# Letting two of the four row groups of a score block start before the running exponential ends, in a scheduled attention plus gated-MLP kernel

## The chip, the cores and the metric

One core of a Trainium2 chip. The metric is the device time of one execution in microseconds (us), as the median of several. Engine names: TensorE (PE in the profile, its weight loads PEld), ScalarE (ACT), VectorE (DVE), GpSimd (POOL), SyncE (SP). In the views, S_ps is the PSUM space of the scores, F_ps that of every other matmul, Pr the probabilities, tnh the outputs of tanh. A wide matmul is one that streams 512 columns.

## The reference, cut to what matters

A transformer layer on 2048 tokens of width 1024: 32 query heads of 32 dimensions share one key head and one value head; then a gated MLP of width 3584.

```python
q = (ln(x) @ wq)            # 2048 x 1024, 32 heads of 32
k, v = ln(x) @ wk, ln(x) @ wv                  # one head each, 2048 x 32
p = softmax(q @ k.T / sqrt(32))                # 32 heads x 2048 x 2048
h = x + (p @ v) @ wo
g, u = ln(h) @ w_gate, ln(h) @ w_up            # 2048 x 3584
out = h + (sigmoid(g) * u) @ w_down            # sigmoid by a tanh on ScalarE
```

## The kernel before

The kernel is written through a list scheduler. Each operation is recorded with the operations that it depends on, an estimated occupancy and latency; the scheduler puts TensorE's work in one fixed order, and the others' with it. On the chip only that order and the semaphore waits exist; the estimates are gone.

The attention part is cut into 512 *score blocks*, 32 for each tile of 128 queries. A block is eight matmuls: four row groups `j` of the array, which run together and hold two heads each, and two rounds `kk` of 128 keys. Six PSUM banks serve the scores as three pairs. Row groups 0 and 1 of block `v` fill one pair and row groups 2 and 3 the next; each pair is read by one exponential of 1024 columns on ScalarE, number `u` = 2v or 2v+1. (The recorded texts below say heads where they mean row groups.)

```python
def t_act(n):                                # the scheduler's idea of a ScalarE instruction
    return dict(occ=n / 1.2 + 53.0, lat=n / 1.2 + 170.0 + SEM)

# s_ready(v): what block v waits for
    deps = [q_ready[qb][g], q_ready[qb][g + 1], k_ev[kq]]
    if 2 * v - 2 >= 0:
        deps.append(exps[2 * v - 2])
    ...
# emit_S(v)
    for kk in range(KB):                     # 2
        for j in range(4):
            bank = 2 * ((2 * v + j // 2) % NB) + j % 2        # NB = 3 pairs
            last = pl.op("pe", mm(S_ps[:, bank, ...], kT4[...], QTb[...], True, True, tile_position=(DH * j, 0)),
                         deps if (kk == 0 and j == 0) else [], occ=27.4, lat=27.4 + 150.0 + SEM)
    for i in range(2):
        u = 2 * v + i
        exps[u] = pl.op("act", ... ACT.activation(out=pslot(slot)..., in_=S_ps[:, pb:pb + 2, :], func=Exp), [last] + free, ...)

# the main loop: a score block goes out when it can, and when ScalarE has under 750 ns of work left
    can_s = sd is not None and known(sd, t)
    if can_s and run - t < 750.0:
        emit_S(v); v += 1
        if pv_fits():
            emit_PV(t)                       # probabilities times values, in column-tiled mode
    # otherwise: matmuls of the projections and of the MLP fill TensorE's time
```

Row groups 0 and 1 of block `v` use the pair that exponential 2v-3 read; row groups 2 and 3 the pair of exponential 2v-2. The whole block waits for 2v-2, while 2v-1 is still running.

The softmax here doesn't subtract the row's maximum and nothing guards it: scores larger than these inputs give would overflow.

## Time and profile before

| | before |
|---|---|
| median | 1092.27 us at first (1091.58 to 1092.71), 1092.13 with the later run |
| ScalarE busy, 581 to 643 us (about one query tile) | 62.00 of 62.00 us |
| end-to-end distance of exponentials | 916.7 ns (mean, 200 to 985 us) |
| period of a query tile | 62.10 us |
| last exponential ends | 1016.5 us |
| rest after it | 72.8 us |

The windows view of the kernel before gives the busy time of each engine in a stretch; the number in brackets counts instructions. The first stretch is one query tile of attention, the second lies in the tail.

```profile
core 0: us, PE busy (x) PEld busy (x) DVE busy (x) ACT busy (x) POOL busy (x), PEclk, DMA share, GB/s
581.00:643.00 62.00, 59.93 (x749) 26.54 (x760) 54.49 (x102) 62.00 (x72) 1.19 (x2) 1.00 0.76 202
1020.00:1089.00 69.00, 65.94 (x328) 29.81 (x326) 15.33 (x28) 4.78 (x8) 0.79 (x2) 1.00 0.78 203
```

ScalarE has no idle time in the first stretch. In the tail it does almost nothing, and TensorE sets the time. The timeline of ScalarE (start, length, then what, and how many instructions were merged) tells its real pace:

```profile
610.92 7.64 ACT L670 ACTIVATE Pr<-S_ps 128x1024 bf16<-128x1024 f32 x8
618.27 0.77 ACT L948 ACTIVATE tnh<-F_ps 128x512 f32<-128x512 f32 x1
618.75 5.80 ACT L670 ACTIVATE Pr<-S_ps 128x1024 bf16<-128x1024 f32 x6
```

Read the ends, not the starts. The eight exponentials end at 610.92 + 7.64 = 618.56, the tanh at 619.04, the next six at 624.55. So a tanh adds about 0.49 us, and an exponential (624.55 - 619.04) / 6 = 0.918 us. The starts overlap the instruction before: the tanh starts 0.29 us before the last of the eight has ended. Unrounded, a tile holds 64 x 0.9167 + 7 x 0.490 = 62.10 us of ScalarE, and the chain of waits repeats every 62.1 us:

```profile
447.98 6.41 ACT Pr L670 x7
510.07 6.42 ACT Pr L670 x7
572.17 6.42 ACT Pr L670 x7
634.26 6.42 ACT Pr L670 x7
```

The waits view of the kernel before (who waited for whom: us in total, times, longest) names the score blocks' wait as a large one:

```profile
PEld S_ps L393 <- ACT Pr L670: 165.8, 388, 0.6
PEld S_ps L393 <- ACT tnh L948: 34.3, 81, 0.4
PEld S_ps L393 <- issue: 14.2, 40, 0.5
```

That is idle time of the weight-load lane, not of the matmuls. Most of it is the 216 ns in which the last wide matmul still streams, and the drain of the array, a further 96 ns between a matmul in another tiling mode and row-tiled ones. From the start of the last wide matmul to the start of the block it takes 311 or 312 ns in 357 of the 475 blocks that follow a wide matmul. Only 103 of the 512 blocks start more than 10 ns later than that, by 9.0 us in all. The counts in this document that no view prints (these waits, end distances, periods) are sums over the records of single instructions.

### The profile page before, as it was taken

The numbers are of one execution on the slowest core, as the hardware profiler recorded it, in microseconds if no ns is written. First come the engines' busy times: TensorE is split into PE (matmuls) and PEld (weight loads), VectorE is DVE, ScalarE is ACT, GpSimd is POOL, SyncE is SP. The second block draws the span as 40 slices with busy tenths as digits, with TensorE's granted clock in tenths as the row PEclk, the third lists the DMA queues.
The fourth block names the chain that finished last, engine by engine and source line by source line (L and its number), as shares of the span: only waits on it lengthen the run. The fifth ranks groups of instructions, "written<-read, shape, count | busy, mean of one in ns | idle before, by whom it ended". The sixth has DMA issues, their size and how long they took to land.

```text
span 1089.3 us, 31275 instructions
## 1 busy us (share of the span) xinstructions
PE 1046.4 (96%) x12757; PEld 481.2 (44%) x12931; DVE 910.2 (84%) x1756; ACT 1006.6 (92%) x1164; POOL 28.5 (3%) x58
## 2 busy tenths in 40 slices
PE   8999999999999999999999999999999999999998
PEld 5664444444444444444444444444444444444443
DVE  8789988898888889798888989898888979888611
ACT  6899999999999999999999999999999999999310
POOL 2100000000000000000000000000000000000000
PEclk9999999999999999999999999999999999999999
DMA  9996599949688694949789594968869494967993
GB/s 251 194 310 221 141 282 256 279 104 281 163 216 231 158 267 113 278 123 261 190 195 256 125 277 106 275 161 235 211 167 260 126 271 115 278 170 196 283 263 89
DMA packets 310991, 228.18 MB, mean 209 GB/s; under 512 B 121920, under 2 KB 302144, under 8 KB 310848
## 3 DMA queue, kind: packets, MB, share of 16 engines
q1 hardware_dynamic: 308768, 226.04, 79.7%
q8 instruction: 102, 1.67, 0.7%
q10 hardware_dynamic: 2080, 0.13, 0.1%
q14 instruction: 41, 0.34, 0.1%
HBM read 195.69 MB, written 7.86 MB: 187 GB/s over the span
## 4 chain that ended last, share of the span: by engine, by line
ACT 47%; PE 31%; issue 10%; DVE 10%; DMA 1%; POOL 0%; SPq 0%; DVEq 0%
ACT Pr L670 41%; PE F_ps L393 27%; ACT tnh L948 5%; DVE Ts L704 5%; PE S_ps L393 5%; DVE Rc L766 1%; DVE h_sb L834 1%; DVE st L334 1%; DVE hact L284 1%; DMA ring<-in_B_w_up_dram 1%; DVE Rc L771 0%; DMA zone<-ring 0%; DMA ring<-in_A_x_dram 0%; DVE Ri L769 0%; ACT wo_sb L670 0%
## 5 line engine op out<-in xcount | busy, mean ns | idle before, releaser
L670 ACT ACTIVATE Pr<-S_ps 128x1024 bf16<-128x1024 f32 x1012 | 962.6, 1177 | 5.9 <-PE S_ps L393 5.8
L704 DVE TENSOR_TENSOR Ts<-Ts,Pr 128x1024 bf16<-128x1024 bf16 x732 | 480.2, 679 | 38.1 <-ACT Pr L670 34.2
L393 PE MATMUL F_ps<-ring,hnT 128*128 128x512 bf16 (+1 forms) x2046 | 411.7, 380 | 19.3 <-issue 12.8
L393 PEld LDWEIGHTS F_ps<-ring,hnT 128*128 128x128 bf16 (+1 forms) x2153 | 156.2, 97 | 194.7 <-issue 50.5
L393 PE MATMUL F_ps<-zone,hact 128*128 128x512 bf16 (+1 forms) x1046 | 212.2, 380 | 7.1 <-issue 4.3
L393 PE MATMUL S_ps<-QTb,kT 32*128 32x256 bf16 x4096 | 203.3, 273 | 3.5 <-ACT Pr L670 0.7
L393 PEld LDWEIGHTS S_ps<-QTb,kT 32*128 32x128 bf16 x4096 | 61.0, 92 | 214.7 <-ACT Pr L670 165.8
L393 PE MATMUL F_ps<-Pr,Vb 128*32 128x256 bf16 x4048 | 134.3, 274 | 0.0
L948 ACT ACTIVATE tnh<-F_ps 128x512 f32<-128x512 f32 x112 | 86.8, 775 | 45.4 <-PE F_ps L393 45.4
L393 PEld LDWEIGHTS F_ps<-zone,hact 128*128 128x128 bf16 (+1 forms) x1088 | 80.9, 97 | 98.6 <-issue 19.6
L704 DVE TENSOR_TENSOR Ts<-Pr 128x1024 bf16<-128x1024 bf16 x126 | 85.9, 683 | 45.0 <-ACT Pr L670 45.0
L393 PEld LDWEIGHTS F_ps<-Pr,Vb 128*32 128x32 bf16 x4048 | 96.3, 96 | 29.9 <-issue 19.0
L952 DVE SCALAR_TENSOR_TENSOR hst<-tnh,F_ps 128x512 bf16<-128x512 f32 x112 | 76.6, 684 | 28.9 <-PE F_ps L393 28.9
L393 PE MATMUL F_ps<-zone 128*128 128x256 bf16 (+4 forms) x574 | 73.5, 274 | 4.3 <-DVE hact L284 1.2
L393 PE MATMUL F_ps<-wo_sb,OT 128*128 128x512 bf16 (+1 forms) x373 | 60.2, 379 | 2.6 <-issue 2.4
L393 PEld LDWEIGHTS F_ps<-zone 128*128 128x128 bf16 (+1 forms) x583 | 41.9, 97 | 27.6 <-issue 9.2
L982 DVE SCALAR_TENSOR_TENSOR h_sb<-F_ps,h_sb 128x512 bf16<-128x512 f32 x32 | 22.1, 692 | 36.4 <-PE F_ps L393 36.4
L711 DVE TENSOR_TENSOR Ts<-Ts 128x1024 bf16<-128x1024 bf16 x64 | 43.9, 686 | 1.5
L348 POOL TENSOR_SCALAR zb<-mvb 128x1 bf16<-128x1 bf16 (+1 forms) x25 | 11.2, 446 | 999.3 <-DVE mvb L344 999.3
L393 PEld LDWEIGHTS F_ps<-wo_sb,OT 128*128 128x128 bf16 (+1 forms) x388 | 22.8, 97 | 26.4 <-issue 6.3
L754 DVE TENSOR_TENSOR Oc<-F_ps,Oc 128x256 f32<-128x256 f32 x60 | 25.4, 424 | 7.0 <-PE F_ps L393 4.5
L771 DVE STREAM_TRANSPOSE Rc<-Ri 128x256 f32<-128x256 f32 x64 | 28.1, 438 | 0.0
(64 smaller groups left out, 345.0 us busy)
## 6 DMA issues: line engine op xcount, KB each, us to landing
ring<-in_B_w_gate_dram SPq DMA_DIRECT2D x320, 256.0 KB, 4.3
ring<-in_B_w_up_dram SPq DMA_DIRECT2D x320, 256.0 KB, 4.3
zone<-in_B_w_down_dram SPq DMA_DIRECT2D x28, 256.0 KB, 3.5
h_sb<-in_A_x_dram SPq DMA_DIRECT2D x16, 256.0 KB, 4.9
out_dram<-h_sb SPq DMA_DIRECT2D x32, 128.0 KB, 3.0
ring<-in_A_x_dram SPq DMA_DIRECT2D x7, 512.0 KB, 6.6
QTb<-q_scratch SPq DMA_DIRECT2D x14, 256.0 KB, 4.2
q_scratch<-hact SPq DMA_DIRECT2D x16, 128.0 KB, 3.1
```

The lines of the kernel that those rows point to most:

```text
L284: lambda: DVE.tensor_copy(out=out_ap, in_=in_ap))
L334: a = pl.op("dve", lambda k=k, src=src: DVE.bn_stats(st[:, k, 0, :], src[:, 0:512]), dep, prio=prio, occ=590, lat=756, order=[st_user.get(k)])
L348: f = pl.op("pool", lambda: POOL.tensor_scalar(out=zb[:, ph, sl].unsqueeze(2), in0=mvb[:, ph, sl, 1:2], scalar1=LN_EPS_BF16, scalar2=None, ...
L393: fn = lambda: PE.matmul(o, lhsT=l, rhs=r, start=start, stop=stop, **kw)
L670: exps[u] = pl.op("act", lambda slot=slot, pb=pb: ACT.activation(out=pslot(slot).rearrange("p (a b) -> p a b", a=2), in_=S_ps[:, pb:pb + 2 ...
L704: o = pl.op("dve", lambda T=T, a=a, b=b: DVE.tensor_tensor(out=T, in0=a, in1=b, op=ALU.add), deps, prio=4, **t_dve(1024, 1.92))
L711: merge_ev[G] = pl.op("dve", lambda T4=T4: DVE.tensor_tensor(out=T4[:, :, 0, :], in0=T4[:, :, 0, :], in1=T4[:, :, 1, :], op=ALU.add), [sum ...
L754: a = pl.op("dve", lambda: DVE.tensor_tensor(out=Oc[:, :], in0=O, in1=Ob, op=ALU.add), [last, oc_ev[G], o_ev.get(G - 1)], prio=0, **t_dve( ...
L771: d = pl.op("dve", lambda: DVE.transpose(out=Rc[:, :], in_=Ri[:, :].unsqueeze(2).to_broadcast([P, 2 * P // DH, DH])), [r], prio=2, **t_dve ...
L948: tanh_of[n] = pl.op("act", lambda: ACT.activation(out=tnh[:, n % 2, :], in_=F_ps[:, b, :], func=ACTF.Tanh, scale=0.5), [last, tn_user.get ...
L952: e = pl.op("dve", lambda: DVE.scalar_tensor_tensor(out=hst[:, n % NST, :], in0=tnh[:, n % 2, :], scalar=1.0, in1=F_ps[:, b, :], op0=ALU.a ...
L982: e = pl.op("dve", lambda: DVE.scalar_tensor_tensor(out=h_sb[:, t % 4, sl], in0=F_ps[:, b, :], scalar=0.5, in1=h_sb[:, t % 4, sl], op0=ALU ...
```

## The change

The intent: the first two row groups need a pair of banks that was read long ago. They should go ahead while the exponential that holds the other pair still runs, and only the third matmul should wait. The scheduler may then send a block up to one drain time (92 to 100 ns by its table) before that exponential ends.

```diff
             deps = [q_ready[qb][g], q_ready[qb][g + 1], k_ev[kq]]
-            if 2 * v - 2 >= 0:
-                deps.append(exps[2 * v - 2])
+            if v > 1:
+                deps.append(exps[2 * v - 3])
@@ emit_S
-                                 deps if (kk == 0 and j == 0) else [], occ=27.4, lat=27.4 + 150.0 + SEM)
+                                 deps if (kk, j) == (0, 0) else [exps[2 * v - 2]] if (kk, j) == (0, 2) and v else [],
+                                 occ=27.4, lat=27.4 + 150.0 + SEM)
@@ main loop
-                can_s = sd is not None and known(sd, t)
+                can_s = sd is not None and known(sd, t) and (v == 0 or known([exps[2 * v - 2]], t + DRAIN[mode[0]]))
```

So there are two parts: semaphores that wait later within a block, and a scheduler rule that makes another order of nearly everything.

## The prediction

> **What bounds the kernel now.** Two engines in turn. Until about 1016.5 us ScalarE sets the pace. In the windows view of 581 to 643 us (one query tile) ScalarE is busy 62.0 of 62.0 us. The starts of exponentials hide the real pace: they lie 904 ns apart with small gaps, but the ends lie 916 to 917 ns apart, and an end after a tanh 490 ns later. The Trainium skill ("Perfetto Trace Analysis", DVE / Act Engine Instruction) says that the recorded end is the write's acknowledgement, so I take the ends; the trace agrees: 64 x 0.9166 + 7 x 0.490 = 62.09 us, and the tile period read from the score blocks is 62.09 us. So in steady state no exponential is late, though score blocks come only just in time. After the last exponential 72.8 us of matmuls remain (512 columns, 216 ns apart): TensorE sets the end. TensorE has work throughout; what it loses in the first part is paid in the tail.
>
> **What the change touches.** A score block follows its predecessor on TensorE by at least 312 ns (216 streaming, 96 drain). "TensorEngine Tiling (Array Packing)", Key Properties, says that a change of tiling mode drains the array; the trace agrees, 96 ns in 80% of blocks. So the weight loads' "wait for the exponential" (165.8 us in the waits view) is mostly drain, which stays. Real waiting beyond 312 ns is only 9 us over 103 of 512 blocks. An exponential just ended lets a block start about 56 ns later; the first two matmuls need only a much older one. But the third still waits for the same end, and the four row groups run together, so starting two early gains little for the block.
>
> The larger effect is that the kernel's list scheduler places blocks up to 96 ns earlier (mostly 35 ns, its 750 ns run-ahead rule binds) and reorders everything. Instruction order, before to after: filler matmuls 38 to 20 (18 x 109 ns, -2.0 us); mode changes 1036 to 1074, because PV groups now often follow full matmuls, not score blocks (about 38 x 0.1 us, +4 us). All transitions summed with measured spacings: TensorE +2.1 us in all. Per steady tile 61.07 becomes 61.39 us, still under ScalarE's 62.09. Work is the same 184 wide matmuls per tile. After the last score block 328 becomes 322 wide matmuls: -1.3 us. One more tanh (104 to 105) comes before the last exponential: +0.5 us.
>
> **Critical path.** The ScalarE period isn't touched, so most of TensorE's saved waiting doesn't count; what counts is the tail (-1.3), the tanh (+0.5) and the first 80 us, where ScalarE idles some 7 us in all and the new order is slightly shorter (-0.5, uncertain). Sum about -1.3 us.
>
> **Prediction: 1091.0 us, range 1087.0 to 1094.5. Chances: faster by over 2% 0.01, within 2% 0.97, slower 0.02.**
>
> **What the profile should show.** Tile period still 62.0 to 62.2 us; ends of exponentials 917 ns apart; drains still 96 ns; TensorE's waits beyond drain before score blocks lower than 9 us, or moved to the third matmul; last exponential within 2 us of 1016.5; tail 70 to 72.5 us; more full-to-column mode changes.
>
> **What would make it wrong.** PV groups now issued when probability slots run out could delay a score block past its slack of some 60 ns and starve ScalarE: period over 62.3 us and end distances over 930 ns. TensorE has only 0.7 us per tile of slack left; other losses (about 0.4 us) could use it up, adding up to 5 us. If the first 80 us lose much of the 7 us idle, it is faster by some 4 us. Weight loads, issued in another order, could stall a matmul by about 2 us, as twice before.

## The result, and the profile after

| | before | after |
|---|---|---|
| median | 1092.13 us (4 runs, 1091.58 to 1092.71) | 1092.05 us (4 runs, 1091.19 to 1092.85) |
| last exponential ends | 1016.5 us | 1019.3 us |
| rest after it | 72.8 us | 71.0 us |
| span of the profiled run | 1089.3 us | 1090.3 us |
| blocks that wait over 10 ns beyond the drain, first matmul | 93, 8.8 us | 1, 0.1 us |
| the same, third matmul | 0 | 110, 7.9 us |

(The row of the first matmul counts from 312 ns on for every block; the 103 blocks above were counted from 311 ns where a full matmul stood before the block, which takes in ten more. The row of the third counts what goes beyond its usual 3 ns after the second.)

The ratio is 0.9999, with a 95% interval from 0.9982 to 1.0016: the same. A ratio is the mean time of one kernel's runs over that of the other's of the same rounds, so it is not quite the ratio of the medians.

The windows view after, for the same stretches:

```profile
581.00:643.00 62.00, 61.94 (x750) 26.67 (x749) 53.78 (x103) 62.00 (x72) 0.79 (x2) 1.00 0.80 203
1020.00:1089.00 69.00, 67.35 (x379) 30.83 (x377) 16.76 (x31) 4.78 (x8) 0.79 (x2) 1.00 0.75 200
```

ScalarE is as full as before. TensorE's busy time seems to grow by 2 us a tile, but it does no more work: the trace of before lacks 174 of the program's 12931 matmul records, that of after none of 12721, and a missing record shows as idle time. In the stretch of before above there are 749 matmuls beside 760 weight loads. `sem_only2`, a run below with the order of before and all its records, shows this for the same stretch:

```profile
581.00:643.00 62.00, 61.82 (x761) 27.04 (x760) 54.61 (x102) 62.00 (x73) 1.19 (x2) 1.00 0.80 203
```

The tail's x328 against x379 is another matter: in after, the last PV group and its sums (36 matmuls) fall behind 1020 us. So neither the busy sum nor the page's chain (ScalarE 47% before, TensorE 86% after) tells of a new limit here; the chain is 90% TensorE in `sem_only2` too.

The timeline of ScalarE after:

```profile
611.36 6.75 ACT L671 ACTIVATE Pr<-S_ps 128x1024 bf16<-128x1024 f32 x7
617.81 0.80 ACT L949 ACTIVATE tnh<-F_ps 128x512 f32<-128x512 f32 x1
618.28 4.90 ACT L671 ACTIVATE Pr<-S_ps 128x1024 bf16<-128x1024 f32 x5
```

The ends are 618.11, 618.61 and 623.18: again 0.50 for the tanh and (623.18 - 618.61) / 5 = 0.914 us for an exponential, the same pace within the rounding. The mean end distance is 916.9 ns, and from the tenth tile on the period is 62.1 us.

The waits view after:

```profile
PEld S_ps L393 <- ACT Pr L671: 114.5, 291, 0.4
PEld S_ps L393 <- issue: 70.2, 187, 0.4
PEld S_ps L393 <- ACT tnh L949: 19.5, 46, 0.4
```

Some 56 us came to the line "issue" (14.2 before, 70.2 after), and the ScalarE lines lost 66 us (165.8 + 34.3 = 200.1 before, 114.5 + 19.5 = 134.0 after): the first weight load no longer has a ScalarE semaphore that came last. Most of the gap stays, because it is the stream and the drain: the three lines sum to 214.3 us before and 204.2 after.

What did change is the start. Before 150 us ScalarE lost 6.7 us between ends in the kernel before and 9.1 us in the kernel after. One stretch alone costs 3.3 us. TensorE's timeline after:

```profile
118.10 0.40 PE L393 MATMUL S_ps<-QTb,kT 32*128 32x256 bf16 x8
118.43 4.06 PE L393 MATMUL F_ps<-zone 128*128 128x512 bf16 x18
122.42 1.06 PE L393 MATMUL F_ps<-Pr,Vb 128*32 128x256 bf16 x32
123.30 0.28 PE L393 MATMUL F_ps<-Ts,ones 128*32 128x256 bf16 x4
123.52 0.40 PE L393 MATMUL S_ps<-QTb,kT 32*128 32x256 bf16 x8
```

and ScalarE's in the same place:

```profile
118.64 2.13 ACT L671 ACTIVATE Pr<-S_ps 128x1024 bf16<-128x1024 f32 x2
123.96 1.02 ACT L671 ACTIVATE Pr<-S_ps 128x1024 bf16<-128x1024 f32 x1 [3.19 <-PE S_ps L393]
```

The order has eighteen projection matmuls and a PV group between two score blocks, 5.4 us, where two exponentials last 1.8 us. In the order of before the same place holds seven projection matmuls, a score block, three more and the PV group:

```profile
117.47 1.68 PE L393 MATMUL F_ps<-zone 128*128 128x512 bf16 x7
119.09 0.40 PE L393 MATMUL S_ps<-QTb,kT 32*128 32x256 bf16 x8
119.64 0.59 PE L393 MATMUL F_ps<-zone 128*128 128x512 bf16 x2 [0.16 <-issue]
120.17 1.06 PE L393 MATMUL F_ps<-Pr,Vb 128*32 128x256 bf16 x32
```

(One of the three is among the missing records; `sem_only2`, with the same order, shows x3.)

### The profile page after: what moved, and what is told of

Read it like the earlier page. It is cut to its first block, busy times and chain, and to the rows that moved or that the text cites. A ratio compares the mean times of both kernels' runs of the same rounds, so it can differ in the third digit from the quotient of the medians.

```text
span 1090.3 us, 31042 instructions
## 1 busy us (share of the span) xinstructions
PE 1077.6 (99%) x12721; PEld 482.6 (44%) x12721; DVE 902.1 (83%) x1756; ACT 1007.3 (92%) x1164; POOL 23.6 (2%) x58
## 4 chain that ended last, share of the span: by engine, by line
PE 86%; ACT 8%; DVE 3%; issue 2%; DMA 1%; POOL 0%; SPq 0%; DVEq 0%
PE F_ps L393 72%; PE S_ps L393 14%; ACT Pr L671 7%; DMA ring<-in_B_w_up_dram 1%; ACT tnh L949 1%; DVE Ts L705 1%; DMA wo_sb<-in_A_wo_dram 0%; DMA ring<-in_A_x_dram 0%; DVE Rc L767 0%; DVE Oc L755 0%; DVE ring L373 0%; DVE ring L380 0%; DVE st L334 0%; DVE st L336 0%; DVE kT L284 0%
## 5 line engine op out<-in xcount | busy, mean ns | idle before, releaser
L393 PE MATMUL F_ps<-ring,hnT 128*128 128x512 bf16 (+1 forms) x1991 | 437.6, 380 | 3.0 <-issue 1.3
L393 PEld LDWEIGHTS F_ps<-ring,hnT 128*128 128x128 bf16 (+1 forms) x1991 | 153.0, 98 | 203.6 <-issue 58.9
L393 PE MATMUL F_ps<-zone,hact 128*128 128x512 bf16 (+1 forms) x1145 | 223.7, 380 | 0.0
L393 PE MATMUL S_ps<-QTb,kT 32*128 32x256 bf16 x4096 | 211.0, 273 | 0.4 <-ACT Pr L671 0.2
L393 PEld LDWEIGHTS S_ps<-QTb,kT 32*128 32x128 bf16 x4096 | 66.7, 92 | 202.9 <-ACT Pr L671 114.5
L393 PEld LDWEIGHTS F_ps<-Pr,Vb 128*32 128x32 bf16 x4048 | 96.4, 96 | 32.6 <-issue 17.6
L393 PE MATMUL F_ps<-zone 128*128 128x256 bf16 (+5 forms) x595 | 74.3, 277 | 4.1 <-DVE Vb L284 0.8
L393 PE MATMUL F_ps<-wo_sb,OT 128*128 128x512 bf16 (+1 forms) x289 | 66.7, 381 | 0.4 <-DMA wo_sb<-in_A_wo_dram 0.4
L348 POOL TENSOR_SCALAR zb<-mvb 128x1 bf16<-128x1 bf16 (+1 forms) x25 | 6.4, 255 | 1006.4 <-DVE mvb L344 1006.4
```

What stands on the lines that cost most here:

```text
L348: f = pl.op("pool", lambda: POOL.tensor_scalar(out=zb[:, ph, sl].unsqueeze(2), in0=mvb[:, ph, sl, 1:2], scalar1=LN_EPS_BF16, scalar2=None, ...
L393: fn = lambda: PE.matmul(o, lhsT=l, rhs=r, start=start, stop=stop, **kw)
```

## The experiments

My theory: ScalarE sets the pace of the attention part, so a block that starts earlier gains nothing; the wait only moves to the third matmul; the reorder costs or gains a little at the two ends. First rival: the early start is worth several us, and the worse order ate them. Second rival: TensorE sets the pace.

All runs of one group share their runs of the kernel before.

### One part at a time

`sem_only2` has the order of before on every engine, with only the semaphores moved:

```diff
-            deps = s_ready(v)
+            deps = [d for d in s_ready(v) if not (v and d is exps[2 * v - 2])] + ([exps[2 * v - 3]] if v > 1 else [])
-                                 deps if (kk == 0 and j == 0) else [], ...
+                                 deps if (kk, j) == (0, 0) else [exps[2 * v - 2]] if (kk, j) == (0, 2) and v else [], ...
```

> The instruction order of the kernel before on every engine, unchanged; only the wait moves: the first two matmuls of a score block wait for the older exponential, the third for the one in progress. Theory (ScalarE paces, the third matmul waits for the same end): 1092.1 us, within 1 us of before; some 90 waits, 8 to 9 us in all, now between the second and third matmul; tile period 62.09 us. Rival (starting two heads early gains, and the new order of the full change ate the gain): 5 to 9 us faster than before, about 1085 us, and the waits largely gone.

`order_only2` has the order of after on every engine, but each block waits whole:

```diff
-                                 deps if (kk, j) == (0, 0) else [exps[2 * v - 2]] if (kk, j) == (0, 2) and v else [],
+                                 deps + ([exps[2 * v - 2]] if v else []) if (kk, j) == (0, 0) else [],
```

> The instruction order of the kernel after on every engine, but every block waits whole, as before the change. Theory: same as after, 1092 us within 1 us; about 90 waits, 8 us, ahead of the first matmul. Rival (early start pays for a worse order): 4 us or more slower than after, 1096 us or more.

Measured: 1091.67 and 1091.52 us, beside 1091.40 us of the kernel before; ratios 1.0000 (0.9987 to 1.0012) and 1.0001 (0.9988 to 1.0014). With `sem_only2`, 122 third matmuls waited 9.3 us in all; with `order_only2`, 102 first matmuls waited 7.3 us. The first rival falls: moving the semaphores alone gains nothing, and undoing them in the new order costs nothing.

One block shows why. The two kernels have the same order, so the same block can be laid side by side. TensorE's timeline of before:

```profile
619.09 0.40 PE L393 MATMUL S_ps<-QTb,kT 32*128 32x256 bf16 x8
619.42 1.47 PE L393 MATMUL F_ps<-ring,hnT 128*128 128x512 bf16 x6
620.93 0.40 PE L393 MATMUL S_ps<-QTb,kT 32*128 32x256 bf16 x8
621.26 1.06 PE L393 MATMUL F_ps<-Pr,Vb 128*32 128x256 bf16 x32
```

and of `sem_only2`:

```profile
619.21 0.40 PE L393 MATMUL S_ps<-QTb,kT 32*128 32x256 bf16 x8
619.53 1.47 PE L393 MATMUL F_ps<-ring,hnT 128*128 128x512 bf16 x6
620.94 0.51 PE L393 MATMUL S_ps<-QTb,kT 32*128 32x256 bf16 x8
621.38 1.06 PE L393 MATMUL F_ps<-Pr,Vb 128*32 128x256 bf16 x32
```

All of `sem_only2` is 0.11 to 0.12 us later here. From the block before, the second block starts 1.84 us later in before and 1.73 us later in `sem_only2`, 0.11 us sooner. But it lasts 0.51 instead of 0.40 us, and the PV group behind it comes 2.17 us after the first block in both. By single records the eight matmuls of that block start at 0, 3, 7, 10, 120, 122, 127, 129 ns in before, and at 0, 4, 118, 121, 124, 128, 237, 241 ns in `sem_only2`. Two row groups run early; the other two and the second round come when they came before, and both exponentials wait for the last matmul of the block.

### More work for one engine

`pe_plus2` repeats the second round of four matmuls in every fourth block, unknown to the scheduler, so that the order stays:

```diff
+            for j in range(4 if v >= 96 and v % 4 == 0 else 0):
+                last = pl.op("pe", mm(<the matmul of kk = 1, row group j, once more>), [], occ=0.0, lat=150.0 + SEM)
```

> The kernel before with the second round of four score matmuls repeated in every fourth block from the fourth tile on (104 blocks, about 110 ns each, 11.4 us of TensorE time in all, 0.88 us a tile), in an otherwise unchanged order. Theory (ScalarE paces the attention part, TensorE waits about 0.9 us a tile): 0 to 3 us slower, tile period 62.1 to 62.3, TensorE's waits ahead of score blocks shrink from about 9 to under 4 us. Rival (TensorE paces): 11 us slower, period 62.9.

`act_plus2` adds a small copy on ScalarE after every eighth exponential:

```diff
+            if v >= 96 and v % 4 == 0:
+                pl.op("act", lambda: ACT.activation(out=scr[:, :], in_=ones[:, :], func=ACTF.Copy), [exps[2 * v], c_v1], prio=0, occ=0.0, lat=0.0)
```

> The kernel before with one small ScalarE copy (128x32) after every eighth exponential from the fourth tile on (104 of them), order otherwise unchanged. From the ends of exponential (916.6 ns, 1024 elements) and tanh (490 ns, 512) I estimate 63 ns fixed plus 0.83 ns an element, so 90 ns each, 9.4 us in all. Theory (ScalarE paces): 8 to 11 us slower, tile period 62.8. Rival (TensorE paces): under 3 us slower.

`act_plus2` took 1101.88 us against 1091.40 (ratio 1.0107, 1.0088 to 1.0126): 10.5 us more for 104 copies. (One of its four runs took 1106.11 us, at a granted clock of 0.998; it lifts the ratio above that of the medians.) Its ScalarE timeline:

```profile
611.28 6.83 ACT L671 ACTIVATE Pr<-S_ps 128x1024 bf16<-128x1024 f32 x7
617.80 0.42 ACT L676 ACTIVATE scr<-ones 128x32 bf16<-128x32 bf16 x1
617.92 4.88 ACT L671 ACTIVATE Pr<-S_ps 128x1024 bf16<-128x1024 f32 x5
```

The ends are 618.11, 618.22 and 622.80. A copy adds 0.11 us (107 ns in the median of all 104; the period rose from 62.10 to 62.95 us with eight copies a tile), though its record is 0.42 us long. So ScalarE's added time is paid in full, 104 x 0.107 = 11.1 us against 10.5 measured.

`pe_plus2` took 1096.41 us (ratio 1.0044, 1.0030 to 1.0058): 5.0 us for 104 x 110 ns = 11.4 us of TensorE work. That is less than half, but more than the 0 to 3 us that I expected. The period became 62.52 us. TensorE's waits ahead of blocks fell to 2.5 us, as expected. The rest is in ScalarE's ends: after 150 us it lost 5.1 us, in pieces of mostly 43 to 120 ns, where before it lost 0.9 us. Of the 56 pieces 42, with 3.8 us, stand at the first exponential of a lengthened block. A TensorE wait of 100 ns at one block cannot pay for 110 ns at another block that is just in time. So TensorE has slack on average and nearly none at some blocks.

### A shorter exponential

Both kernels with exponentials over 992 of 1024 columns. The result is wrong (relative error 0.217); the order stays on every engine but for two fills on GpSimd that give the missing columns a value.

```diff
-                    out=pslot(slot).rearrange("p (a b) -> p a b", a=2), in_=S_ps[:, pb:pb + 2, :],
+                    out=pslot(slot).rearrange("p (a b) -> p a b", a=2)[:, :, 0:496], in_=S_ps[:, pb:pb + 2, 0:496],
```

> Wrong result on purpose: every exponential of the kernel before does 992 of 1024 columns, order unchanged on every engine but for two small fills at the start. ScalarE is then 26.7 ns shorter per exponential (32 x 0.833), 27 us in all, and its tile period would be 60.4 us. Theory (ScalarE paces, TensorE's 61.07 us of work and drains a tile are the next limit): period 61.1 to 61.5 us, total 1079 to 1084 us, TensorE's waits ahead of score blocks under 3 us. Rival (TensorE or memory traffic paces already): within 2 us of before.

> The same shortening of every exponential in the kernel after, order unchanged, wrong result on purpose. Theory: with TensorE as the limit its longer sum counts (61.39 against 61.07 us a tile, 2.1 us more in all), so 1 to 4 us slower than the shortened kernel before. Rival (the early start is worth something once ScalarE is out of the way): 2 us or more faster than the shortened kernel before.

Measured: 1082.27 us for the shortened before (ratio to the kernel before 0.9910, 0.9896 to 0.9923) and 1082.40 us for the shortened after (0.9917, 0.9903 to 0.9930), beside 1092.11 us. ScalarE's timeline in `less_before`:

```profile
613.56 0.62 ACT L951 ACTIVATE tnh<-F_ps 128x512 f32<-128x512 f32 x1
614.03 5.48 ACT L673 ACTIVATE Pr<-S_ps 128x992 bf16<-128x992 f32 x6
```

From 614.18 to 619.51 six exponentials end 0.888 us apart. Taking 27 us off ScalarE takes 9.8 us off the kernel; then ScalarE begins to lose time (17.6 us after 150 us), and TensorE's waits ahead of blocks shrink to 0.2 us. So the second rival falls too, but the next limit lies only 0.5 us a tile below the first: period 61.56 us. Here, with TensorE as the limit, the change as a whole is still worth nothing: the two are 0.1 us apart in the medians. The early start alone was not run with shortened exponentials; but where the blocks of `less_before` wait only 0.2 us in all, it has next to nothing to save. My expectation that the order of after would be 1 to 4 us slower here isn't borne out either: its steady period is 61.48 us, 0.08 shorter, not 0.32 longer, and only its start is longer.

### The right pace in the scheduler

The scheduler counts 53 ns of fixed cost for a ScalarE instruction; both the exponential and the tanh fit 63.3 ns (916.7 - 853.3 = 63.4, and 490 - 426.7 = 63.3). Both kernels with that figure:

```diff
-    return dict(occ=n / 1.2 + 53.0, lat=n / 1.2 + 170.0 + SEM)
+    return dict(occ=n / 1.2 + 63.3, lat=n / 1.2 + 170.0 + SEM)
```

> The kernel before with the scheduler's fixed cost of a ScalarE instruction set from 53 to the measured 63.3 ns; it makes another order. Steady tile 61.07 us of TensorE, tail 70.7 against 72.2 us, but 2.8 us more TensorE work in all and more of it in the first tiles. Theory (ScalarE paces the steady part, which the order can't change): period 62.1, total 1088 to 1095 us. Rival (score blocks wait because the scheduler's clock for ScalarE is too fast, so the right figure pays): 1084 us or less.

> The kernel after with the same 63.3 ns. The 18 matmuls in a row that starved ScalarE for 3.3 us at 121 us are gone from the order; the tail is 72.2 us again; TensorE's sum is 1057.9 us, the least of the four. Theory: period 62.1, last exponential 2 to 4 us earlier than in the kernel after, total 1087 to 1092 us. Rival as in the run before: 1084 us or less.

Measured: 1091.23 us (ratio 0.9993, 0.9981 to 1.0006) and 1091.25 us (0.9992, 0.9980 to 1.0004), beside 1092.11: the same. Two more orders, and the attention part keeps its pace. This table puts the profiled runs together (ScalarE's loss: by how much exponentials and tanhs ended later than 917 and 490 ns after the end before them, in the shortened kernels 890 and 490, summed where it is over 30 ns; the period is that of the tenth tile on):

```
run           period  ScalarE loss   last exp.   rest    span
                      before 150 us  ends
before         62.10    6.7          1016.5      72.8   1089.3
after          62.10    9.1          1019.3      71.0   1090.3
sem_only2      62.10    7.0          1016.6      72.8   1089.4
order_only2    62.10    8.5          1018.3      71.0   1089.3
before_633     62.10    8.7          1017.5      73.6   1091.1
after_633      62.10    6.8          1015.9      73.1   1089.0
pe_plus2       62.52    6.4          1021.2      72.9   1094.1
act_plus2      62.95    6.3          1026.2      72.8   1099.0
less_before    61.56    8.5          1007.9      73.1   1081.0
less_after     61.48   10.7          1009.3      71.3   1080.6
```

`after_633` has the rule of the change, but not the eighteen matmuls in a row, and its start loses 6.8 us, as before's does with 6.7. So the loss at the start belongs to one order, not to the rule. A single run's start also varies: at 42 us ScalarE loses 1.7 us in before and 2.3 us in `sem_only2`, with the same order.

## Why the prediction was right

- **ScalarE sets the pace of the attention part: right, and shown.** Four orders of real work run at 62.1 us a tile in the steady part; 107 ns more on ScalarE costs 107 ns; 27 us less gains 9.8 us, until TensorE limits.
- **The third matmul still waits for the same end, so the block gains little: right, and shown** by the two halves of the change, each within 0.0002 of before in its ratio, and by the record times of one block. The wait moved as forecast: 8.8 us ahead of the first matmul became 7.9 us ahead of the third.
- **Drains stay: right.** The usual distance from a wide matmul to a block is 311 or 312 ns in `sem_only2` and after as in before.
- **The tail gets 1.3 us shorter and one more tanh costs 0.5 us.** The rest after the last exponential fell by 1.8 us in the profiled runs, and in `order_only2` too. The order of after does have 105 tanhs ahead of the last exponential where before has 104, but no run separates the cost of that one.
- **"the first 80 us, where ... the new order is slightly shorter (-0.5, uncertain)": right as far as it looked, but it stopped too early.** Up to 80 us ScalarE's loss fell from 5.65 to 5.19 us. From 80 to 150 us it rose from 1.10 to 3.90 us: eighteen matmuls between two score blocks starved ScalarE for 3.3 us, in a stretch that the prediction's path left out. So the start as a whole lost 2.3 us more in after (1.7 in `order_only2`), and the last exponential ended 2.8 us later, outside the forecast "within 2 us of 1016.5". The order is fixed when the kernel is built, so a listing of it could have shown the eighteen matmuls before any run.
- **"TensorE +2.1 us in all" and 61.39 against 61.07 us a tile** are sums over the order, and were right not to be counted in the attention part. As a forecast of TensorE's pace they fail: in the shortened kernels the period was 0.08 us shorter, not 0.32 longer.
- **TensorE's slack of 1 us a tile** is real as a sum, but half of the work put into it came out again as time.
- The sum, -1.3 us, can't be told from the measured -0.1 us: the interval of the ratio is about 1.8 us to either side. That the total came so near is partly luck: the tail gained more than forecast (1.8 us) and the start lost what was not forecast (2.3 us), and the two nearly cancel.
- The feared losses didn't come: PV groups after full matmuls (9 changes from full to column-tiled mode in the order of before, counted in `sem_only2`, and 48 in after) did not starve ScalarE in the steady part (after 150 us it lost 0.7 us, against 0.9 us before).

What stays open: why TensorE's period in the shortened kernels is 61.5 us and not 61.1 or 61.4; the rest may be bank waits, which no run separated.

## What to carry to other kernels

When the waiting engine is not the one that sets the pace, letting it start earlier only moves its wait. Find the pace first from the ends of the instructions on the full engine, and count how much of a listed wait is a drain that stays anyway. With a list scheduler, test a rule and a semaphore separately: each can be built with the other's order held fixed, and a change of rule must also be read for long runs of other work between two instructions that feed the full engine.

## What the Trainium skill lacked or had wrong

- "ScalarE: Activation LUTs", What ACT_TABLE_LOAD costs, gives an ACTIVATE with immediate scale and bias as 186 ns plus 0.833 ns an element, and an overlap of about 93 ns back to back. Taken together, an estimate from that page, each one in an unbroken row adds 93 ns plus 0.833 ns an element. Here, by the ends, it is 63 ns plus 0.833 ns an element for exponential (1024 columns, 916.7 ns) and tanh (512, 490 ns) that read PSUM, and 107 ns, or 80 ns plus the columns, for a copy of 32 columns in SBUF whose record is some 430 ns long. The slope agrees; the fixed part is smaller, and differs between the two cases.
- "Perfetto Trace Analysis", DVE / Act Engine Instruction, explains start and end but not which to take for a pace. On ScalarE the starts of exponentials are mostly 903 or 904 ns apart while the ends are 916.7 ns apart: the records grow from 1063 to 1337 ns within a tile and shrink where a start comes late. The starts show gaps of 40 to 125 ns where the ends show no loss.
- "TensorEngine Tiling (Array Packing)", Key Properties, says that a change of mode drains the array, without a figure. Here it is 96 ns beyond the stream of the last matmul from full to row-tiled.
- "Perfetto Trace Analysis" warns, in its opening note, that matmul busy time is no measure of the limit, because matmuls are pipelined. 174 of 12931 matmul records are missing in one trace, and TensorE's busy time in the same 62 us falls with them from 61.82 us (`sem_only2`, complete, the same order) to 59.93 us.
